# Hourglass attention and an ELU layer: a constant loaded ahead of v, v in 102-row transfers, two halves at the end of batch 0, and wider filling matmuls

## The chip, the cores and the metric

The kernel runs on one core of one Trainium2 chip. TensorE (PE) multiplies matrices into PSUM, VectorE (DVE), ScalarE (ACT) and GpSimd (POOL) do the elementwise work, SyncE (SP) and POOL issue transfers between DRAM and the core's memory. The metric is device time in microseconds for one execution. Profiles are of one execution each.

## The reference

The inputs q, k and v are 8 batches x 8 heads x 576 tokens x 64, float32. Each head has two attentions, added: one over tokens pooled by four, repeated back to 576, and one over a band of seven tokens. The result, laid out as 4608 x 512, goes through a two-matrix layer with ELU.

```python
q_d = q.reshape(B, H, Sd, factor, D).mean(axis=3)      # k_d, v_d likewise
out_up = np.repeat(sm_attn(q_d, k_d, v_d), factor, axis=2)
mask = np.abs(pos[:, None] - pos[None, :]) < factor    # factor = 4
scores = np.where(mask, scale * np.matmul(q, k.transpose(0, 1, 3, 2)), -1e9)
...
attn_out = out_up + np.matmul(softmax(scores), v)
h = x @ w_in                                           # x: 4608 x 512, w_in: 512 x 2048
return np.where(h > 0.0, h, np.exp(np.minimum(h, 0.0)) - 1.0) @ w_out
```

## The kernel before

Work is fp16 on PE with float32 sums. A batch is four pairs of heads. A pair is loaded (`load`, SP), cast to fp16 (`cast`, mostly POOL; the fp16 copies rotate through 4 buffers), transposed and pooled by matmuls (`transposes`), and multiplied to scores (`scores`): 576 tokens are six blocks of 96 queries, each against 102 keys (96 and three neighbours on either side), and the pooled 144. ACT takes the exponential, DVE applies the mask. `denominators` sums them by matmuls with an indicator matrix, DVE takes the reciprocal, and the reciprocals are then spread over 128 partitions: for batches 0 and 1 (`BY_PE`) by matmuls with the constant SEL (in the tile CC) and a copy by ACT; for the others by a transfer to DRAM and two back that repeat it (POOL). `pool_v` pools v by matmuls; `outputs` multiplies probabilities with v (L738) and pooled v (L746) into two banks, DVE multiplies by the reciprocals (xn, L755), and POOL, in batch 0 partly DVE, adds the local and the repeated pooled part into `xt`, blocks of 512 tokens that the layer reads.

The layer runs over nine blocks of 512 tokens: `mm1` (sixteen steps of four 512-column matmuls, L788; exponential on ACT, minimum and maximum on DVE) and `mm2` (four output rows, each in four steps of four matmuls, L811). A step needs its slice of w_in (five transfers w0 to w4) or of w_out (w5 to w8).

v lies in a tile of 102 partitions, so that block c of a head holds tokens 96c-3 to 96c+98 of its rows. For batches 1 to 7 POOL issues two halo transfers of 3 partitions x 48 blocks (L467) and two main ones of 96 partitions x 24 blocks (L422), which cast on the way. For batch 0, SP loads float32 (two halos L440 and L442, four main transfers of 96 partitions x 12 blocks L445) into a buffer lent by `gt`, and POOL casts (L450, vc00 to vc03).

The order of all this is written by a planner in the file (`Plan`): every operation has an engine, an assumed duration, a rank, and buffers; the planner runs a clock, lets each engine take the ready operation of lowest rank that has its buffers, and models transfers by an assumed rate. Ranks come from `PARAM`. The resulting order is then issued as it stands: on the chip each engine runs its list in that order, and waits where something is missing. Where the planner has nothing for PE before `FILL` = 37 us of its own clock, it puts a filling matmul (L337) of zeros into bank 7; these are instructions like others. The first 57 are ahead of the first transposes.

Every output, score or transpose takes a pair of banks ("two"): one of four pairs in batch 0, one of two pairs later. SP has eight transfers in flight at most; the next waits for the one eight before it.

```python
plan.zero = plan.op("DVE", 0.15, -99, lambda: nc.vector.memset(zero[:], 0.0), name="zero")
c_a = consts((("ONE", one_np), ("BY6", by6_np), ("VR", vr_np)), "CA", -60)
c_b = consts((("MASK", m2_np), ("IND", ind_np), ("SEED", seed_np)), "CB", -47.5)
c_c = consts((("SEL", sel_np),), "CC", -45.0)
```

Of the kernel before, what the change touches and what calls it, by code (L numbers as in the profile page):

```python
# [10 lines left out]
FP16 = mybir.dt.float16  # L11
# [7 lines left out]
NB, QB = 6, 96  # L19
# [66 lines left out]
class Plan:  # L86
# [63 lines left out]
    def run(self):  # L150
# [38 lines left out]
        while n < len(self.ops):  # L189
            for e, todo in ready.items():  # L190
                if busy[e] > now + 1e-9 or not todo and e != "PE":
                    continue
                if e == "SP" and len(lanes) >= 8 and lanes[-8].done is None:
                    continue
                full = e == "POOL" and sum(x[1] for x in queues["POOL"]) > self.depth
                todo.sort(key=lambda o: (o.rank, o.i))
                for o in todo:
                    if o.nbytes and full:
                        continue
                    got = []  # L200
                    for b in o.bufs:
                        if b.slot is None:
                            x = self._take(b, free)
                            if x is None:
                                break
                            self._hold(b, x, free)
                            got.append(b)
                    else:
                        break
                    for b in reversed(got):  # L210
                        self._drop(b, free, True)
                else:
# [54 lines left out]
    def emit(self):  # L267
        for o in self.order:
# [7 lines left out]
MOE_BANKS = {"hp": 3, "op": 2}  # L276
PARAM = dict(M0=43.0, P=36.0, LAG=0.84, LEAD=48.6, GAP=6.2, SC=2.7, DEN=29.4, OUT=8.8, OUTG=1.0, TV=18.4, LOAD=11.5,
             VLOAD=3.4, V1=2, warm=3.4, FILL=37.0, DEPTH=12.0, WI=-44.0, WO=43.8, WOG=2.5)


@with_exitstack
def kernel(
# [50 lines left out]
    plan.warm, plan.depth, plan.fill = PARAM["warm"], PARAM["DEPTH"], PARAM["FILL"]  # L333
    zero = sb.tile([128, 256], FP16, tag="zero", name="zero")

    def fill():
        nc.tensor.matmul(PS[:, 7, 384:512], zero[:, 0:128], zero[:, 128:256], start=True, stop=True)  # L337

# [76 lines left out]
    def load_v(b):  # L415
# [4 lines left out]
        def main(h):  # L420
            t = at(x)[3 : 3 + QB].rearrange("p j e c d -> p (j e c) d")
            nc.gpsimd.dma_start(  # L422
                out=t[:, 24 * h : 24 * h + 24, :],
                in_=bass.AP(tensor=a.tensor, offset=a.offset + 24 * h * QB * D, ap=[[D, QB], [QB * D, 24], [1, D]]),
            )

# [3 lines left out]
        if b == 0:  # L430
# [5 lines left out]

            def halos0(left):
                if left:
                    nc.vector.memset(flat()[0:3, 0:1, :], 0.0)
                    nc.sync.dma_start(out=flat()[0:3, 1:48, :], in_=blocks(1, 48, -3, 3))  # L440
                else:
                    nc.sync.dma_start(out=flat()[99:KW, :, :], in_=blocks(0, 48, QB, 3))  # L442

            def main0(j):
                nc.sync.dma_start(  # L445
                    out=flat()[3 : 3 + QB, 12 * j : 12 * j + 12, :], in_=blocks(12 * j, 12 * j + 12, 0, QB)
                )

            def cast0(j):
# [3 lines left out]

            hs = [op("SP", 0.45, r, lambda i=i: halos0(i), writes=[x32], nbytes=3 * 48 * 256, rate=100e3, name=f"vh{i}")
                  for i in range(2)]
            for j in range(NPAIR):
                o = op("SP", 0.45, r + 0.1, lambda j=j: main0(j), writes=[x32], nbytes=96 * 768 * 4, rate=205e3, packet=20, name=f"vm0{j}")
                plan.op("POOL", 0.85, r + 0.2, lambda j=j: cast0(j), writes=[x32, x], after=[o] + hs, name=f"vc0{j}")
                st.setdefault("vc", []).append(plan.ops[-1])
            st[b] = x  # L460
# [3 lines left out]

        def halo(p, tok, lo, hi):
            t = at(x)[p : p + 3].rearrange("p j e c d -> p (j e c) d")
            nc.gpsimd.dma_start(out=t[:, lo:hi, :], in_=blocks(lo, hi, tok, 3))  # L467

        def halos():
            t = at(x)  # L470
            if b == B - 1:
                nc.gpsimd.memset(t[96:KW, 3, 1, NB - 1, :], 0.0)
            halo(0, -3, 0, 48)
            halo(99, QB, 0, 47 if b == B - 1 else 48)

        pre = [wq[int(PARAM["V1"])]] if b == 1 else [wq[-1]]
        op("POOL", 1.6, r, halos, writes=[x], after=pre, nbytes=6 * 48 * 256, rate=60e3, packet=28, name=f"vh{b}")
        for h in range(2):
            op("POOL", 1.0, r + 0.1 + 0.1 * h, lambda h=h: main(h), writes=[x], after=pre, nbytes=96 * 24 * 256,
               rate=146e3, packet=28, name=f"vm{b}{h}")  # L480
# [4 lines left out]
    def weights(i):  # L485
        wi = i < 5
        if wi:
            lo, hi = WIC[i], WIC[i + 1]
            src = moe_w_in.rearrange("(c p) m -> p c m", p=128)[:, :, lo:hi]
            to, r, n = WI[:, :, lo:hi], PARAM["WI"] + 0.1 * i, hi - lo  # L490
        else:
            n = 4 * (i - 5)
            src = moe_w_out.rearrange("(c p) m -> p c m", p=128)[:, n : n + 4, :]
            to, r, n = WO[:, n : n + 4, :], PARAM["WO"] + PARAM["WOG"] * (i - 5), 512
        o = op("POOL", 1.3, r, lambda: nc.gpsimd.dma_start(out=to, in_=src), name=f"w{i}", after=[st["vc"][GATES[i]]],
               nbytes=128 * 16 * n, rate=330e3)
# [81 lines left out]
    def pool_v(b, j):  # L578
        s, r = st[b, j], out_rank(b) - PARAM["TV"] + j
        yv = st[b]  # L580
# [12 lines left out]
        w = Buf("vd")  # L593
        eng = "ACT" if b == 0 else "DVE"
        op(eng, 0.41, r + 0.1,
# [4 lines left out]
    def scores(b, j):  # L600
        s, r = st[b, j], late(b, j) + PARAM["SC"]
        m = b in SIX
# [38 lines left out]

    stR = {}

    def denominators(b, js):
        last = js[-1] == NPAIR - 1
        if b == 0:
            r = late(b, js[-1]) + PARAM["SC"] + 1.0
        else:
            r = M0 + P * b - PARAM["DEN"]
# [33 lines left out]
        if b in BY_PE:  # L683
# [3 lines left out]
            for j in js:  # L687
                w = Buf("two", b < EARLY)

                def spread(j=j, w=w):  # L690
# [9 lines left out]

                op("PE", 0.35, out_rank(b) - 1 + 0.1 * j, spread, reads=[c], writes=[w], after=[c_c], name=f"spr{b}{j}")
                op("ACT", 0.76, out_rank(b) - 0.9 + 0.1 * j,
                   lambda j=j, w=w: nc.scalar.copy(out=at(y)[:, j], in_=two(w, 0, 128, 0, GW)),
                   reads=[w], writes=[y], name=f"evr{b}{j}")
# [24 lines left out]
    def outputs(b, j):  # L729
        s, r = st[b, j], out_rank(b) + PARAM["OUTG"] * j  # L730
        x, vd, v16, y = s["ex"], s["vd"], st[b], stR[b, j]
        z, w = Buf("two", b < EARLY), Buf("xn")

        def go():
# [8 lines left out]
            for h in range(2):  # L743
# [142 lines left out]
```

## Time and profile before

| what | us |
|---|---|
| median of 3 runs (378.05, 380.81, 380.75) | 380.75 |
| the profiled execution | 379.33 |
| its span | 377.6 |
| PE busy (96% of the span) | 362.2 |
| of it mm1 and mm2 (1152 matmuls) | 146.8 + 144.8 |
| of it filling matmuls (173) | 19.3 |
| DVE, ACT, POOL busy | 226.0, 206.9, 144.1 |
| transfers | 44.06 MB, mean 117 GB/s |

A busy PE is not PE at its peak: matmuls are pipelined, so the duration of one (381 ns for 512 columns) is longer than its share of the time when many follow each other (0.86 us for four). PEclk is the clock that PE was granted, as a fraction. The DMA share is the mean busy share of 16 DMA engines; it can read over 1 where transfers overlap. Lines of the profile are `start, length, engine, line, operation, out<-in, count`, with the idle time before it and what ended it in brackets.

### The profile page before, as it was taken

The page shows a single profiled execution, that of the slowest core. Times are in us where ns is not written, and L with a number is a line of the kernel's source. Part 1 is how long each engine was busy: PE and PEld are TensorE (multiplying, and loading weights), DVE is VectorE, ACT ScalarE, POOL GpSimd, SP SyncE. Part 2 cuts the span into 40 slices and gives each one's busy share as a digit, 9 for nine tenths or more (in the row PEclk, how much of TensorE's full clock was granted, in tenths as well). Part 3 has the DMA queues.
Part 4 walks back from the last instruction along what each step waited for, and adds up shares of the span by engine and source line. Part 5 has one row for each costly group of instructions (what it writes and reads, how often), then busy time and mean ns, then how long its engine had stood idle before and what let it go on. Part 6 is the DMA issues. An engine that isn't in the chain of part 4 may idle for free.

```text
span 377.6 us, 9204 instructions
## 1 busy us (share of the span) xinstructions
PE 362.2 (96%) x3805; PEld 205.2 (54%) x3805; DVE 226.0 (60%) x407; ACT 206.9 (55%) x353; POOL 144.1 (38%) x225
## 2 busy tenths in 40 slices
PE   8969999999988999999999999999999999999995
PEld 8857855654644554555555555555555444444442
DVE  2623397847737665866576657665756675655530
ACT  2732489658452946494749474947494334443421
POOL 1282782199116813770387038703700240000000
PEclk9975699999998999999999999999999999999999
DMA  8999999929981997299729973924000401010012
GB/s 220 178 239 217 207 183 186 199 42 201 194 182 32 152 137 168 70 143 135 169 77 139 134 168 82 99 42 106 30 30 33 115 29 48 28 56 30 28 56 84
DMA packets 119740, 44.06 MB, mean 117 GB/s; under 512 B 105779, under 2 KB 113907, under 8 KB 119699
## 3 DMA queue, kind: packets, MB, share of 16 engines
q1 hardware_dynamic: 69971, 30.22, 35.3%
q0 software_dynamic: 49728, 13.26, 31.5%
q8 instruction: 29, 0.48, 0.5%
q14 instruction: 12, 0.10, 0.1%
HBM read 42.36 MB, written 9.66 MB: 138 GB/s over the span
## 4 chain that ended last, share of the span: by engine, by line
PE 83%; DMA 8%; DVE 3%; SPq 3%; ACT 2%; issue 1%; POOL 0%; DVEq 0%; ACTq 0%
PE bank L811 33%; PE bank L788 31%; PE bank L544 4%; PE bank L586 3%; PE bank L738 3%; DMA ld<-in_k_dram 3%; PE bank L658 2%; PE bank L612 2%; SPq L445 2%; DMA ld<-in_q_dram 2%; DMA rcb<-rd 2%; DMA CC<-CCc 1%; PE bank L337 1%; PE bank L746 1%; DVE e L796 1%; ACT ex L629 1%
## 5 line engine op out<-in xcount | busy, mean ns | idle before, releaser
L788 PE MATMUL bank<-xt,WI 128*128 128x512 f16 x576 | 146.8, 381 | 1.0 <-DVE gt L799 1.0
L811 PE MATMUL bank<-WO,gt 128*128 128x512 f16 x576 | 144.8, 381 | 0.0
L794 ACT ACTIVATE e<-bank 128x512 f16<-128x512 f32 x144 | 85.9, 600 | 89.8 <-PE bank L788 68.3
L799 DVE SCALAR_TENSOR_TENSOR gt<-bank,e 128x512 f16<-128x512 f32 x144 | 98.8, 689 | 5.2
L796 DVE TENSOR_SCALAR e<-e 128x512 f16<-128x512 f16 x144 | 54.4, 378 | 56.8 <-ACT e L794 56.2
L811 PEld LDWEIGHTS <-gt 128*128 128x128 f16 x576 | 53.6, 98 | 59.6 <-issue 0.3
L788 PEld LDWEIGHTS <-WI 128*128 128x128 f16 x576 | 52.7, 98 | 58.0 <-issue 2.6
L512 POOL CAST c<-ld 96x768 f16<-96x768 f32 x60 | 51.1, 868 | 46.8 <-issue 26.0
L629 ACT ACTIVATE ex<-bank 102x864 f16<-102x864 f32 x64 | 53.4, 887 | 21.8 <-PE bank L620 21.7
L771 POOL TENSOR_TENSOR xt<-xn 128x288 f16<-128x288 f16 (+8 forms) x92 | 44.8, 516 | 52.0 <-DVE xn L755 51.9
L637 DVE TENSOR_TENSOR ex<-ex,CB 102x1152 f16<-102x1152 f16 x32 | 25.1, 785 | 30.0 <-ACT ex L629 29.3
L755 DVE TENSOR_TENSOR xn<-bank,rcb 128x720 f16<-128x720 f32 x32 | 28.7, 903 | 15.3 <-DMA rcb<-rd 4.7
L826 ACT COPY os<-bank 128x512 f32<-128x512 f32 x36 | 21.1, 590 | 15.8 <-PE bank L811 15.7
L544 PEld LDWEIGHTS <-c 96*128 96x128 f16 x288 | 19.5, 99 | 10.2 <-issue 1.3
L559 ACT CAST qt<-bank 128x720 f16<-128x720 f32 x24 | 18.2, 757 | 10.8 <-PE bank L544 10.2
L544 PE MATMUL bank<-CA,c 96*128 96x120 f16 x288 | 23.0, 217 | 0.0
L708 POOL DMA_DIRECT2D rd<-rc x6 | 3.5, 582 | 49.1 <-DVE rc L681 49.1
L337 PE MATMUL bank<-zero 128*128 128x128 f16 x173 | 19.3, 280 | 1.9 <-DVE zero L340 1.1
L738 PE MATMUL bank<-ex,v 102*64 102x96 f16 x384 | 14.9, 218 | 4.2 <-DVE xn L755 3.7
L738 PEld LDWEIGHTS <-v 102*64 102x64 f16 x384 | 11.0, 116 | 13.0 <-issue 12.6
L570 ACT CAST kt<-bank 128x576 f16<-128x576 f32 x24 | 15.5, 646 | 4.2 <-PE bank L544 2.8
L596 DVE CAST vd<-bank 72x256 f16<-72x256 f32 x28 | 11.5, 416 | 9.9 <-PE bank L586 9.9
(47 smaller groups left out, 265.0 us busy)
## 6 DMA issues: line engine op xcount, KB each, us to landing
ld<-in_q_dram SPq DMA_DIRECT2D x32, 288.0 KB, 5.5
ld<-in_k_dram SPq DMA_DIRECT2D x32, 288.0 KB, 6.1
out_dram<-os SPq DMA_DIRECT2D x36, 256.0 KB, 2.1
rcb<-rd POOLq DMA_DIRECT2D x12, 360.0 KB, 5.1
v<-in_v_dram POOLq DMA_DIRECT2D x14, 288.0 KB, 7.6
WO<-in_moe_w_out_dram POOLq DMA_DIRECT2D x4, 512.0 KB, 16.0
WI<-in_moe_w_in_dram POOLq DMA_DIRECT2D x3, 512.0 KB, 16.7
gt<-in_v_dram SPq DMA_DIRECT2D x4, 288.0 KB, 8.2
```

The source lines that it names most:

```text
L512: f(out=at(y)[:], in_=at(x)[:].rearrange("p e c d -> p c e d"))
L544: nc.tensor.matmul(o, t[:, c, :, :], C["ONE"], start=True, stop=True)
L629: lambda e=e: nc.scalar.activation(out=at(x)[:, e], in_=two(sc[e], 0, KW, 0, HB + SD), func=AF.Exp, scale=SCALE),
L637: nc.vector.tensor_tensor(out=a, in0=a, in1=mk, op=AB.mult)
L738: nc.tensor.matmul(PS[64 * e : 64 * e + 64, z.slot[0] + c // 3, QB * (c % 3) : QB * (c % 3) + QB], v_[:, j, e, c, :], ex[:, e, c // 3, QB ...
L755: lambda: nc.vector.tensor_tensor(out=at(w)[:], in0=two(z, 0, 128, 0, GW), in1=at(y)[:, j], op=AB.mult),
L771: (nc.vector if eng == "DVE" else nc.gpsimd).tensor_tensor(out=at(xt(t))[:, j, o : o + n - a], in0=ln, in1=gn, op=AB.add)
L788: nc.tensor.matmul(one(h, 0, 128, 0, TBLK), WI[:, dc, 128 * fc : 128 * fc + 128], at(x)[:, dc, :], start=(dc == 0), stop=(dc == DMC - 1),)
L794: op("ACT", 0.55, r, lambda: nc.scalar.activation(out=at(e)[:], in_=one(h, 0, 128, 0, TBLK), func=AF.Exp), reads=[h], writes=[e], name=f"e ...
L796: op("DVE", 0.36, r, lambda: nc.vector.tensor_scalar(out=at(e)[:], in0=at(e)[:], scalar1=1.0, scalar2=-1.0, op0=AB.min, op1=AB.add), reads ...
L799: op("DVE", 0.69, r, lambda: nc.vector.scalar_tensor_tensor(out=at(gt)[:, fc, :], in0=one(h, 0, 128, 0, TBLK), scalar=0.0, op0=AB.max, in1 ...
L811: nc.tensor.matmul(one(z, 0, 128, 0, DM), at(gt)[:, fc, 128 * tt : 128 * tt + 128], WO[:, fc, :], start=(fc == 0), stop=(fc == FCN - 1),)
```

## The change

Eight edits, all but the last in what the planner is given:

- CC is ranked directly behind CB, ahead of the last pair of q and k of batch 0 and of v.
- v of batch 0: the four main transfers start three tokens earlier and fill partitions 0 to 95 (first block left out of the first); one transfer of 6 partitions x 47 blocks brings the rest, two small ones the first block. v of batches 1 to 7: no halos; two transfers of 102 partitions x 24 blocks (the last batch's last block apart, by one more).
- Batch 0's end: the spreads of pairs 0 and 1 come ahead of the scores of pair 3; the four v-poolings stand together, the copies of the first two on DVE instead of ACT; the outputs of pairs 0 and 1 come ahead of the second half of the denominators, those of pairs 2 and 3 behind it.
- Filling matmuls have 256 columns instead of 128; the planner takes 0.112 us for each instead of 0.107. 158 instead of 173 are issued, 54 instead of 57 of them ahead of the first transposes.
- POOL's transfers over 400 KB wait until its queue holds less than 2 us of work (12 before, and any transfer then). w3 goes behind the first four adds of batch 0, w4 behind the rest of them and two casts, w5 to w8 behind casts of batch 2.
- The reciprocals' trip through DRAM is modelled by bytes instead of fixed delays.
- Ranks: see PARAM. Besides, xn now enters the planner as a writer of `rcb`.
- The order that results: scores of batch 1's first pair follow the first two mm1 steps instead of preceding them; the v-poolings of batch 1 stand directly behind its denominators, ahead of its spreads; the first mm2 step follows mm1's sixteenth instead of its ninth. For batch 2, four blocks of mm1 and mm2 stand between its first and second output, and nine between the second and the third.

```diff
-                    if o.nbytes and full:
+                    if o.nbytes > 400000 and full:
...
-                        o = Op("PE", 0.107, 0, self.filler, "fill")
+                        o = Op("PE", 0.112, 0, self.filler, "fill")
...
-PARAM = dict(M0=43.0, P=36.0, LAG=0.84, LEAD=48.6, GAP=6.2, SC=2.7, DEN=29.4, OUT=8.8, OUTG=1.0, TV=18.4, LOAD=11.5,
-             VLOAD=3.4, V1=2, warm=3.4, FILL=37.0, DEPTH=12.0, WI=-44.0, WO=43.8, WOG=2.5)
+PARAM = dict(M0=33.0, P=36.0, LAG=0.84, LEAD=50.2, GAP=5.6, SC=2.5, DEN=29.4, OUT=8.8, OUTG=0.9, TV=15.0, LOAD=22.0,
+             VLOAD=14.6, V1=2, warm=3.4, FILL=37.0, DEPTH=2.0, WI=-44.0, WO=41.2, WOG=2.1)
...
-    zero = sb.tile([128, 256], FP16, tag="zero", name="zero")
+    zero = sb.tile([128, 384], FP16, tag="zero", name="zero")
...
-        nc.tensor.matmul(PS[:, 7, 384:512], zero[:, 0:128], zero[:, 128:256], start=True, stop=True)
+        nc.tensor.matmul(PS[:, 7, 256:512], zero[:, 0:128], zero[:, 128:384], start=True, stop=True)
...
-    c_c = consts((("SEL", sel_np),), "CC", -45.0)
+    c_c = consts((("SEL", sel_np),), "CC", -47.0)
...
+    def spr_rank(b, j):
+        if b == 0:
+            return -30.5 + 0.1 * j if j < 2 else -27 + 0.1 * j
+        return out_rank(b) - 1 + 0.1 * j
...
         def main(h):
-            t = at(x)[3 : 3 + QB].rearrange("p j e c d -> p (j e c) d")
...
+            t = at(x)[:].rearrange("p j e c d -> p (j e c) d")
+            hi = 24 * h + 24
...
+            nc.gpsimd.dma_start(out=t[:, 24 * h : hi, :], in_=blocks(24 * h, hi, -3, KW))
...
+            def first():
+                nc.vector.memset(flat()[0:3, 0:1, :], 0.0)
+                nc.sync.dma_start(out=flat()[3:99, 0:1, :], in_=blocks(0, 1, 0, QB))
+
+            def last():
+                nc.sync.dma_start(out=flat()[96:KW, 1:48, :], in_=blocks(1, 48, 93, 6))
+                nc.sync.dma_start(out=flat()[99:KW, 0:1, :], in_=blocks(0, 1, QB, 3))
...
-                nc.sync.dma_start(
-                    out=flat()[3 : 3 + QB, 12 * j : 12 * j + 12, :], in_=blocks(12 * j, 12 * j + 12, 0, QB)
-                )
+                lo = max(12 * j, 1)
+                nc.sync.dma_start(out=flat()[0:QB, lo : 12 * j + 12, :], in_=blocks(lo, 12 * j + 12, -3, QB))
...
-        op("POOL", 1.6, r, halos, writes=[x], after=pre, nbytes=6 * 48 * 256, rate=60e3, packet=28, name=f"vh{b}")
...
-            to, r, n = WI[:, :, lo:hi], PARAM["WI"] + 0.1 * i, hi - lo
+            to, r, n = WI[:, :, lo:hi], PARAM["WI"] if i < 3 else -25.0, hi - lo
...
-        s, r = st[b, j], out_rank(b) - PARAM["TV"] + j
+        s, r = st[b, j], out_rank(b) - PARAM["TV"] + j if b else -29.5 + 0.1 * j
...
-        eng = "ACT" if b == 0 else "DVE"
+        eng = "ACT" if b == 0 and j > 1 else "DVE"
...
-            r = late(b, js[-1]) + PARAM["SC"] + 1.0
+            r = late(b, js[-1]) + 2.8 if js[0] == 0 else -28.5
...
-               reads=[c], writes=[d], name=f"spo{b}").lag = 3.0
+               reads=[c], writes=[d], name=f"spo{b}", nbytes=36864, rate=100e3, packet=30)
...
-                op("POOL", 0.8, r + 1.1, lambda e=e: spread(e), reads=[d], writes=[y], name=f"spi{b}{e}").lag = 4.0
+                op("POOL", 0.8, r + 1.1, lambda e=e: spread(e), reads=[d], writes=[y], name=f"spi{b}{e}", nbytes=64 * 4 * 1440, rate=200e3, packet=90)
...
-        s, r = st[b, j], out_rank(b) + PARAM["OUTG"] * j
+        s, r = st[b, j], out_rank(b) + PARAM["OUTG"] * j if b else (-29 if j < 2 else -26) + 0.1 * j
...
-           reads=[z, y], writes=[w], name=f"xn{b}{j}")
+           reads=[z], writes=[w, y], after=[evr[b, j]] if b in BY_PE else y.writers, name=f"xn{b}{j}")
```

More of the change, by code (lines that the diff above doesn't have):

```diff
@@ L420, in main @@
         def main(h):
-            t = at(x)[3 : 3 + QB].rearrange("p j e c d -> p (j e c) d")
-            nc.gpsimd.dma_start(
-                out=t[:, 24 * h : 24 * h + 24, :],
-                in_=bass.AP(tensor=a.tensor, offset=a.offset + 24 * h * QB * D, ap=[[D, QB], [QB * D, 24], [1, D]]),
-            )
+            t = at(x)[:].rearrange("p j e c d -> p (j e c) d")
+            hi = 24 * h + 24
+            if b == B - 1 and h == 1:
+                hi -= 1
+                nc.gpsimd.memset(t[96:KW, hi, :], 0.0)
+                nc.gpsimd.dma_start(out=t[0:99, hi : hi + 1, :], in_=blocks(hi, hi + 1, -3, 99))
+            nc.gpsimd.dma_start(out=t[:, 24 * h : hi, :], in_=blocks(24 * h, hi, -3, KW))
         def blocks(lo, hi, tok, n):
@@ L435, in flat @@
                 return t.rearrange("p (c d) -> p c d", d=D)
[L437 to L442, printed above, removed]
+            def first():
[4 more added lines that the diff above has]
+                nc.sync.dma_start(out=flat()[99:KW, 0:1, :], in_=blocks(0, 1, QB, 3))
             def main0(j):
-                nc.sync.dma_start(
-                    out=flat()[3 : 3 + QB, 12 * j : 12 * j + 12, :], in_=blocks(12 * j, 12 * j + 12, 0, QB)
-                )
+                lo = max(12 * j, 1)
+                nc.sync.dma_start(out=flat()[0:QB, lo : 12 * j + 12, :], in_=blocks(lo, 12 * j + 12, -3, QB))
             def cast0(j):
@@ L452, in cast0 @@
                 )
-            hs = [op("SP", 0.45, r, lambda i=i: halos0(i), writes=[x32], nbytes=3 * 48 * 256, rate=100e3, name=f"vh{i}")
-                  for i in range(2)]
+            hs = [
+                op("SP", 0.9, r, last, writes=[x32], nbytes=6 * 48 * 256, rate=150e3, name="vh0"),
+                op("SP", 0.45, r, first, writes=[x32], nbytes=96 * 256, rate=150e3, name="vh1"),
+            ]
             for j in range(NPAIR):
-                o = op("SP", 0.45, r + 0.1, lambda j=j: main0(j), writes=[x32], nbytes=96 * 768 * 4, rate=205e3, packet=20, name=f"vm0{j}")
+                o = op("SP", 0.45, r + 0.1, lambda j=j: main0(j), writes=[x32], nbytes=96 * 768 * 4, rate=175e3, packet=20, name=f"vm0{j}")
                 plan.op("POOL", 0.85, r + 0.2, lambda j=j: cast0(j), writes=[x32, x], after=[o] + hs, name=f"vc0{j}")
+                plan.ops[-1].lag = 0.8
                 st.setdefault("vc", []).append(plan.ops[-1])
@@ L463, in load_v @@
             return
[L465 to L474, printed above, removed]
         pre = [wq[int(PARAM["V1"])]] if b == 1 else [wq[-1]]
-        op("POOL", 1.6, r, halos, writes=[x], after=pre, nbytes=6 * 48 * 256, rate=60e3, packet=28, name=f"vh{b}")
         for h in range(2):
-            op("POOL", 1.0, r + 0.1 + 0.1 * h, lambda h=h: main(h), writes=[x], after=pre, nbytes=96 * 24 * 256,
+            op("POOL", 1.0, r + 0.1 + 0.1 * h, lambda h=h: main(h), writes=[x], after=pre, nbytes=KW * 24 * 256,
                rate=146e3, packet=28, name=f"vm{b}{h}")
@@ L494, in weights @@
             to, r, n = WO[:, n : n + 4, :], PARAM["WO"] + PARAM["WOG"] * (i - 5), 512
-        o = op("POOL", 1.3, r, lambda: nc.gpsimd.dma_start(out=to, in_=src), name=f"w{i}", after=[st["vc"][GATES[i]]],
+        o = op("POOL", 0.8, r, lambda: nc.gpsimd.dma_start(out=to, in_=src), name=f"w{i}", after=[st["vc"][GATES[i]]],
                nbytes=128 * 16 * n, rate=330e3)
@@ L600, in scores @@
     def scores(b, j):
-        s, r = st[b, j], late(b, j) + PARAM["SC"]
+        s, r = st[b, j], late(b, j) + (PARAM["SC"] if b else 2.7)
         m = b in SIX
@@ L640, in scores @@
         s["ex"] = x
-    stR = {}
+    stR, evr = {}, {}
     def denominators(b, js):
@@ L699, in spread @@
                         )
-                op("PE", 0.35, out_rank(b) - 1 + 0.1 * j, spread, reads=[c], writes=[w], after=[c_c], name=f"spr{b}{j}")
-                op("ACT", 0.76, out_rank(b) - 0.9 + 0.1 * j,
+                op("PE", 0.35, spr_rank(b, j), spread, reads=[c], writes=[w], after=[c_c], name=f"spr{b}{j}")
+                evr[b, j] = op("ACT", 0.76, spr_rank(b, j),
                    lambda j=j, w=w: nc.scalar.copy(out=at(y)[:, j], in_=two(w, 0, 128, 0, GW)),
```

## The prediction

> **What bounds the kernel now.** I read the page first, then the chain of waits, then busy time by window, then the engine timeline at the two places the windows point to. The page says the tensor engine is the bound almost throughout; what it does not say is whether it is busy with useful work. Two lines of the 40 slices (9.4 us each) do:
>
> ```profile
> PE   8969999999988999999999999999999999999995
> PEclk9975699999998999999999999999999999999999
> ```
>
> The clock is low only in slices three to five (19 to 47 us) and a little in slice thirteen. By windows (PE, weight loads, DVE, ACT, POOL busy, granted clock, DMA share, GB/s):
>
> ```profile
> 20.00:22.00 2.00, 0.00 (x0) 0.00 (x0) 0.37 (x2) 1.66 (x2) 1.61 (x3) 1.00 1.20 256
> 22.00:24.00 2.00, 0.36 (x5) 0.37 (x6) 0.57 (x1) 0.00 (x0) 1.51 (x2) 0.94 1.08 234
> 24.00:26.00 2.00, 2.00 (x21) 1.78 (x19) 0.00 (x0) 0.12 (x1) 2.00 (x4) 0.50 1.07 258
> ...
> 112.00:114.00 2.00, 0.00 (x0) 0.00 (x0) 0.00 (x0) 0.11 (x1) 0.00 (x0) 1.00 0.35 119
> 114.00:116.00 2.00, 0.85 (x22) 0.68 (x22) 1.81 (x3) 0.00 (x0) 0.82 (x2) 0.98 0.01 3
> 116.00:118.00 2.00, 2.00 (x11) 1.04 (x10) 2.00 (x4) 0.00 (x0) 2.00 (x5) 0.50 0.00 0
> ```
>
> Twice the tensor engine stands still for over 3.5 us, and each time the clock is 0.50 afterwards: from 24 to 44.5 us, and from 116 to about 119.5. From 120 to 360 us it is busy for 240.00 of 240 us, so whatever is lost before 120 us is lost for good, and nothing but that is to be had. The chain of waits and the PE timeline name the two causes (start, length, what):
>
> ```profile
> 16.91 1.81 SPq L445
> 18.76 4.83 DMA CC<-CCc
> ...
> 107.93 6.13 DMA rcb<-rd
> ```
> ```profile
> 1.06 6.01 PE L337 MATMUL bank<-zero 128*128 128x128 f16 x57 [1.06 <-DVE zero L340]
> 18.30 1.11 PE L337 MATMUL bank<-zero 128*128 128x128 f16 x17 [0.41 <-DVE rc L681]
> 23.64 0.71 PE L696 MATMUL bank<-rc,CC 32*128 32x144 f16 x6 [3.69 <-DMA CC<-CCc]
> 31.78 1.57 PE L337 MATMUL bank<-zero 128*128 128x128 f16 x13
> 115.15 0.45 PE L738 MATMUL bank<-ex,v 102*64 102x96 f16 x12 [3.67 <-DVE xn L755]
> ```
>
> The first spread sits in PE's queue waiting for its constant CC, which SP issues only after four v transfers; everything behind it, fillers too, waits. The second stop is batch 2's outputs waiting for the reciprocals' trip through DRAM. The first mm1 starts at 44.64 us, after 20 us at half clock.
>
> **Part by part.**
>
> *CC ahead of v.* It is issued after CB, so by about 5 us. CB took 8.5 us to land (at 12.6); CC is right behind it with 160 KB at some 230 GB/s, so there by 13.5 us, before the first spread (its reciprocal ends at 18.25). The 3.69 us stop goes. The last q and k of batch 0 (the cast that waits for them starts at 15.81) and v are pushed back by these 0.7 us; v ends where CC ended, at about 23.6.
>
> *v of batch 0 without halos.* Two transfers of 3 rows x 48 pieces become one of 6 x 47, one of 3 and one of 96. The four main issues took 9.50 us on SP, so the queue was full and it, not SP, is the limit. The casts start at 18.63, 19.72, 21.14 and 23.29, about 1.6 us for 72 pieces on each of 16 engines. If a row stays on one engine, the halos put 95 pieces on three engines and now 48 on six: 0 to 1.0 us sooner. I take 0, since nothing shows which engines; the last cast ends at about 24.5.
>
> *Fillers of 256 columns.* This has a price. Four 512-column matmuls take 0.86 us at full clock, 216 ns each; so a 256-column one is 108 ns at full and 216 at half clock. The first 57 of 128 columns took 6.01 us, 105 ns each, against 65 for the 17 at 18.30: they ran at half speed, though the clock column shows 1.00 there. Of the 54 new ones, 27 fit into the 5.84 us that the old ones took to 6.9 us, and 27 x 0.108 = 2.9 us follow. The first transposes start at 9.8 instead of 6.9. The bounds are 0 (full speed from the start) and 5.8 us (half speed throughout).
>
> *From there to the first mm1.* In the new order PE runs without a hole: 10 transposes at 0.60, 4 scores at 0.50, 2 half denominators at 1.0, 4 spreads at 0.36, 4 v-poolings at 0.32 (1.28 for two at half clock), 4 outputs at 0.42, and 104 fillers at 0.108: 6.0 + 2.0 + 2.0 + 1.4 + 1.3 + 1.7 + 11.2 = 25.6 us, with 0.4 for hand-overs 26.0; mm1 at 35.8. Is anything later than that? PE reaches the first v-pooling at 9.8 + 4.8 + 2.0 + 1.0 + 0.7 + 75 x 0.108 = 26.4, the casts end at 24.5: covered by 1.9 us. The two copies moved to DVE (0.42 each) stand behind the last mask, due at about 26, and end at 27.2, where PE gets to outputs at 27.7. POOL's adds end at 35. So 44.64 becomes 35.8; one scores step of batch 1 (0.5) is moved behind mm1. Gain 8.3 us.
>
> *Weights on POOL.* w1 and w2 follow one cast more, w3 and w4 come behind adds (issue at about 32 and 38 instead of 25.5 and 26.3). The queue held the five for 11.6 to 19.5 us, w4 landing at 45.8; mm1 needs its part (the thirteenth block, 18 us after the first in the trace) at 35.8 + 18 = 54. Nothing lost. The output weights go behind casts of batch 2, about 55 to 68 us, one every 3 to 4 us, needed from 64 on; at 7 us to landing for the first (44.19 before, behind w4) they are in time by 1 to 3 us. I take 0, up to 3.
>
> *v of batches 1 to 7.* Four POOL issues (2 x 0.77 + 2 x 1.20 us) become two; POOL has room, so the 1.5 us are worth nothing. What matters is landing. For batch 1 the second transfer is behind a cast that waits for a buffer of the third pair, so at about 48 us; the v-pooling of batch 1 moved ahead of the spreads and needs it at 35.8 + 24 = 60. Twelve us, where the trace shows:
>
> ```profile
> v<-in_v_dram POOLq DMA_DIRECT2D x14, 288.0 KB, 7.6
> ...
> rd<-rc POOLq DMA_DIRECT2D x6, 36.0 KB, 1.8
> ...
> v<-in_v_dram POOLq DMA_DIRECT2D x13, 18.0 KB, 3.6
> ```
>
> and 12.5 as the longest, in just this stage. A row of 3 partitions with 144 pieces takes twice as long as one of 128 partitions with 128 pieces and twice the bytes: how the rows divide over the engines counts. For 102 rows no row exists. Bounds: 0 (7.6 us) and 11 us (the third rival). I take 1.0 us, nearest to the 96-row transfers.
> The Trainium skill, DMA: Bandwidth & Descriptors (Why a DMA increments its semaphore by 16 and not by 1), says a transfer uses the largest number of engines up to 16 that divides the rows, which is 16 for 96 and 6 for 102, with an exception that gives some POOL copies 16. By the rule the third rival's 390 would come out; by the exception (7 rows on most engines) the sum would stand.
>
> *Reciprocals of batch 2.* In the new order ten mm blocks of 0.87 us, four v-poolings and a scores step stand on PE between batch 2's denominators and its first output (10.5 us), and thirteen blocks and two transposes between that and the output that needs a bank back from xn (11.9), where there were three blocks. Less 1.1 for DVE's reciprocal, PE needs the reciprocals 21 us after they are made. They took 14.4 us, from 99.67 to landing at 114.06. The 3.67 us stop goes, and with it the half clock: 2 us at 0.50 and 2 at 0.67 cost 1.0 + 0.7. Gain 5.4 us. What is late next: batch 3, where PE has only about the 8.3 us of that trip (140.11 to 148.44); 0 to 2, I take 0.5.
>
> *Between.* Without an mm2 block among them, the 16 mm1 go at ACT's pace (per pair 2 x 0.89 + 1.9 + 4 x 0.60 = 6.1 us against 5.2 on PE): 1.0 lost, 0 to 2.
>
> Sum: 8.3 + 5.4 - 1.0 - 0.5 - 1.0 = 11.2 us. The profiled execution took 379.33 (span 377.6), the median of the runs is 380.75: 368.1 and 369.5. I say 369.
>
> **Rivals.**
>
> *The clock falls all the same.* If v's casts end 3.5 us later than PE gets to them (at 30 instead of 24.5), PE stops there and all to mm1 runs at half clock; from 27 to 36 that is some 9 us more, less what the fillers covered: about 377. For it: the DMA share is over 1.0 all that time, and SP sees v later. Against: v moves no more bytes.
>
> *The reciprocals' stop stays*, since the trip in POOL's queue now has a v transfer between its two halves: 5.4 are not gained, 374.4. Against: the 21 us, which would leave 7 for it.
>
> *Slower: v of batch 1 lands on few engines.* From the rows above, 48 pieces on an engine cost 3.6 - 1.8 us more than 8: 46 ns each. 144 pieces give 6.6 + 1.8 = 8.4, near the 7.6 seen. If the rows were divided evenly, 102 would go to 6 engines (17 each): 408 pieces give 20.6 us. Then v of batch 1 at 69, PE stopped for 9 us and at half clock after (1.7); batch 2, with 12 us as well, the same: 369 + 2 x 10.7 = 390. It decides from about 12 us to landing; each us over that is one lost. Against: in the quiet stages the 3-row transfers landed in 2.6 us, which makes a piece much cheaper.
>
> *It does less than it says*: with all fillers at half speed at the start and the output weights 3 us late, 369 + 2.9 + 3 = 375.
>
> **How the numbers follow.** Forecast 0.60, at 363.5 to 372.5: down by 2.9 with the first fillers at full speed, 1.5 with no new waits and 1.0 with v sooner; up by 3 with the fillers or the output weights at their dear end. The clock 0.10, the reciprocals 0.09, few engines 0.11, less than it says 0.10. A difference below 1% (3.8 us) can hardly be told from none here. Faster by over 1% (under 377): 0.60 + 0.09, half of the clock's 0.10, and 0.06 of the last, the rest of which meets another loss: 0.80. Within 1%: 0.05 + 0.04 = 0.09. Slower: 0.11. The range, 363.5 to 376.5, holds all that lies under 377.
>
> **What would show it.** Right: no PE stop over 1 us and a clock of 1.00 from 10 to 120 us; first transposes at 8.5 to 10; mm1 at 34 to 37; no stop at 111; v of batch 1 in under 12 us. Wrong: the L586 group or L811 waiting for a DMA near 60 to 70 us, a half clock in slices three to five, or xn waiting for rcb in batch 2 or 3.

## The result, and the profile after

The change makes the kernel slower, by more than it was forecast to gain.

| kernel | median us | lowest to highest | ratio to before, 95% |
|---|---|---|---|
| before (same chip, 4 runs) | 379.80 | 378.05 to 380.81 | |
| changed (4 runs) | 395.00 | 393.71 to 400.51 | 1.039 [1.032, 1.047] |

The slowest run of the changed kernel, 400.51 us, was in a slower state of the chip and is not in the ratio.

The profiled execution took 393.71 us (span 391.7), 14.4 more than the one of before. The first mm1 starts at 41.21 instead of 44.64, so 3.4 us are gained by then. From there to the end of the last matmul it takes 346.7 us instead of 329.05: 17.7 are lost in the part that the change was least expected to touch. On the page, PE and its clock in 40 slices (9.8 us each):

```profile
PE   8998997899699999599979899999999999999996
PEclk9998999699999999799989999999999999999999
```

Of the low clock in slices three to five one dip is left, in slice 4 (counted from 1). New are the holes of PE in slices 7, 11, 17 and 21; but for slice 11, a low clock stands in the same slice or the next. The PE timeline says what stands there; its last bracket is the idle time ahead of the line and what ended it:

```profile
34.19 2.15 PE L337 MATMUL bank<-zero 128*128 128x256 f16 x10 [1.69 <-DVE rc L679]
...
67.90 0.97 PE L584 MATMUL bank<-v,CA 102*72 102x128 f16 x12 [2.03 <-DMA v<-in_v_dram]
...
71.20 1.87 PE L809 MATMUL bank<-WO,gt 128*128 128x512 f16 x4 [1.39 <-DMA ld<-in_q_dram]
...
104.50 0.86 PE L584 MATMUL bank<-v,CA 102*72 102x128 f16 x12 [3.42 <-DMA v<-in_v_dram]
...
162.21 0.69 PE L736 MATMUL bank<-ex,v 102*64 102x96 f16 x12 [4.14 <-DVE xn L753]
...
201.07 0.47 PE L542 MATMUL bank<-CA,c 96*128 96x120 f16 x6 [2.30 <-DVE xn L753]
```

(Two lines have gone from the code, so L586, L738, L788, L811 and L755 of before are L584, L736, L786, L809 and L753 here.) v of batch 1 is late at 68 us and v of batch 2 at 104; the reciprocals of batches 3 and 4 are late at 162 and 201; where there was a stop of 3.67 us for batch 2's reciprocals at 115, there is none. The line at 71.20 is a first mm2 step. The page names a load of q, but the first of the output weights, issued by POOL at 59.1, landed at 71.1, and that is what this step needs.

With one of 1.20 us at 223 the stops behind the first mm1 add up to 14.5 us where there were 3.7, which is 10.8 more. The half clock at these places adds up to 17.1 us where there were 3.4; 2.9 of the 17.1 lie inside the stops at 71 and 162. A microsecond at half clock loses at most half of itself, so this costs up to (17.1 - 2.9 - 3.4) / 2 = 5.4 more. Together that is 16.2 of the 17.7. By windows (columns as before) this is how such a place looks:

```profile
66.00:68.00 2.00, 0.10 (x2) 0.10 (x3) 0.25 (x1) 1.58 (x2) 0.00 (x0) 1.00 1.28 191
68.00:70.00 2.00, 1.81 (x24) 1.35 (x24) 1.51 (x4) 0.38 (x1) 0.00 (x0) 0.63 1.22 197
70.00:72.00 2.00, 0.80 (x2) 0.36 (x3) 0.80 (x2) 1.04 (x2) 0.00 (x0) 0.50 1.22 201
```

PE has nothing to do, the DMA engines are busy throughout, and POOL does nothing; it had issued the second v transfer of batch 1 by 55.6 us. The wait is for the transfer, not for its issue. In the page's DMA parts a queue has its packets, MB and share, and an issue its count, KB each and median us to landing. First a queue of the kernel before:

```profile
q0 software_dynamic: 49728, 13.26, 31.5%
```

The same queue after, and two rows of issues:

```profile
q0 software_dynamic: 97760, 13.46, 38.1%
...
v<-in_v_dram POOLq DMA_DIRECT2D x13, 306.0 KB, 14.5
WO<-in_moe_w_out_dram POOLq DMA_DIRECT2D x4, 512.0 KB, 13.6
```

q0 is POOL's queue. It moves 1.5% more bytes in twice as many packets, and v takes 14.5 us to land where the main transfers took 7.6. POOL is held longer by each issue too, 2.54 us instead of 1.20. What goes the same way behind v pays as well: the chain of waits (start, length, what) has

```profile
88.12 16.34 DMA v<-in_v_dram
...
155.42 5.71 DMA rcb<-rd
...
187.50 5.72 DMA rd<-rc
...
194.14 5.84 DMA rcb<-rd
```

rd<-rc moves 36 KB and had a median of 1.8 us. Batch 4's is issued at 187.5 while the v transfer of 174.1 is on its way; v lands at 193.0 and rd<-rc at 193.2. Batch 3's was issued at 148.3 behind one of 135.8 that landed at 153.5, and landed at 154.5.

### The profile page after: what moved, and what is told of

It reads as the page before. It is cut to its first block, busy times and chain, and to the rows that moved or that the text cites. A ratio compares the mean times of both kernels' runs of the same rounds, so it can differ in the third digit from the quotient of the medians.

```text
span 391.7 us, 9156 instructions
## 1 busy us (share of the span) xinstructions
PE 367.8 (94%) x3790; PEld 203.7 (52%) x3790; DVE 233.6 (60%) x409; ACT 207.8 (53%) x351; POOL 155.2 (40%) x212
## 3 DMA queue, kind: packets, MB, share of 16 engines
q0 software_dynamic: 97760, 13.46, 38.1%
## 4 chain that ended last, share of the span: by engine, by line
PE 73%; DMA 14%; DVE 5%; issue 4%; ACT 2%; POOL 1%; DVEq 0%; ACTq 0%; POOLq 0%
PE bank L809 29%; PE bank L786 24%; PE bank L337 5%; DMA v<-in_v_dram 4%; DMA ld<-in_q_dram 3%; PE bank L542 3%; DMA rcb<-rd 3%; PE bank L736 3%; DMA out_dram<-os 2%; PE bank L610 2%; PE bank L584 2%; DVE e L794 2%; DMA rd<-rc 1%; PE bank L656 1%; DVE xn L753 1%
## 5 line engine op out<-in xcount | busy, mean ns | idle before, releaser
L809 PE MATMUL bank<-WO,gt 128*128 128x512 f16 x576 | 148.2, 387 | 3.1 <-DMA ld<-in_q_dram 1.4
L786 PE MATMUL bank<-xt,WI 128*128 128x512 f16 x576 | 145.1, 380 | 1.6 <-DVE gt L797 1.5
L794 DVE TENSOR_SCALAR e<-e 128x512 f16<-128x512 f16 x144 | 58.9, 410 | 59.6 <-ACT e L792 59.1
L809 PEld LDWEIGHTS <-gt 128*128 128x128 f16 x576 | 53.8, 99 | 62.8 <-issue 5.7
L786 PEld LDWEIGHTS <-WI 128*128 128x128 f16 x576 | 53.8, 98 | 62.4 <-issue 4.0
L769 POOL TENSOR_TENSOR xt<-xn 128x288 f16<-128x288 f16 (+8 forms) x92 | 46.0, 527 | 47.3 <-DVE xn L753 47.0
L627 ACT ACTIVATE ex<-bank 102x864 f16<-102x864 f32 x64 | 53.5, 889 | 10.8 <-PE bank L618 10.6
L753 DVE TENSOR_TENSOR xn<-bank,rcb 128x720 f16<-128x720 f32 x32 | 28.7, 903 | 31.2 <-PE bank L744 19.0
L432 POOL DMA_DIRECT2D v<-in_v_dram x14 | 35.5, 2538 | 7.9 <-issue 7.8
L337 PE MATMUL bank<-zero 128*128 128x256 f16 x158 | 24.2, 307 | 3.2 <-DVE rc L679 2.1
L542 PE MATMUL bank<-CA,c 96*128 96x120 f16 x288 | 21.9, 216 | 2.5 <-DVE xn L753 2.3
L542 PEld LDWEIGHTS <-c 96*128 96x128 f16 x288 | 18.4, 97 | 11.0 <-issue 2.8
L337 PEld LDWEIGHTS <-zero 128*128 128x128 f16 x158 | 16.2, 109 | 7.3 <-issue 2.4
L584 PE MATMUL bank<-v,CA 102*72 102x128 f16 x192 | 14.3, 221 | 5.4 <-DMA v<-in_v_dram 5.4
L736 PE MATMUL bank<-ex,v 102*64 102x96 f16 x384 | 14.9, 217 | 4.1 <-DVE xn L753 4.1
## 6 DMA issues: line engine op xcount, KB each, us to landing
v<-in_v_dram POOLq DMA_DIRECT2D x13, 306.0 KB, 14.5
```

Source lines behind the costliest of these rows:

```text
L337: nc.tensor.matmul(PS[:, 7, 256:512], zero[:, 0:128], zero[:, 128:384], start=True, stop=True)
L432: nc.gpsimd.dma_start(out=t[:, 24 * h : hi, :], in_=blocks(24 * h, hi, -3, KW))
L542: nc.tensor.matmul(o, t[:, c, :, :], C["ONE"], start=True, stop=True)
L627: lambda e=e: nc.scalar.activation(out=at(x)[:, e], in_=two(sc[e], 0, KW, 0, HB + SD), func=AF.Exp, scale=SCALE),
L753: lambda: nc.vector.tensor_tensor(out=at(w)[:], in0=two(z, 0, 128, 0, GW), in1=at(y)[:, j], op=AB.mult),
L769: (nc.vector if eng == "DVE" else nc.gpsimd).tensor_tensor(out=at(xt(t))[:, j, o : o + n - a], in0=ln, in1=gn, op=AB.add)
```

## The experiments

The first theory was that the rows are the cause: 102 is 6 x 17, so that v of batches 1 to 7 goes over few engines in long runs, everything in POOL's queue waits, and PE's stops follow. The rival was that the loss lies in the rest of the change, its order at the end of batch 0, its wide fillers and its later weights, with v only one of several late things. Each run below was timed beside runs of the kernel before: their median was 378.82 us for the first four experiments and 376.60 for the next four, and the last stands beside a single run of 377.20.

**The changed kernel with 112 rows.** Ten rows more than anybody reads; 112 is 16 x 7. VW is 112 and KW stays 102; what reads v takes rows 0 to 101, and those lines are left out here.

```diff
-        "v16": many("v16", [KW, NPAIR, 2, NB, 64]),
+        "v16": many("v16", [VW, NPAIR, 2, NB, 64]),
...
-            nc.gpsimd.dma_start(out=t[:, 24 * h : hi, :], in_=blocks(24 * h, hi, -3, KW))
+            nc.gpsimd.dma_start(out=t[:, 24 * h : hi, :], in_=blocks(24 * h, hi, -3, VW))
```

> The changed kernel, order untouched, but each v transfer of batches 1 to 7 has 112 rows instead of 102 (ten more rows of following tokens that nothing reads; 112 is 7 x 16). Theory 1, the row count: 102 rows are what makes a v transfer slow, so although 10% more bytes move, landing falls from 14.5 us to 8 to 9, POOL's issue of one from 2.5 us to about 1.3, packets in POOL's queue from 97,760 to about 53,000, and the stops at 68, 104, 162 and 201 us with the half clock behind them go: 395 - 2.0 - 3.4 - 4.1 - 2.3 - 1.4 - 7.0 for the half clock = about 375. Theory 2, the order: v is slow because of where it is issued, among loads and weights; 10% more bytes make it worse, 395 or more, landing 14.5 us or more.

Measured: 371.75 us, 0.983 [0.979, 0.986]. One number in a transfer's shape, with 10% more bytes, is worth 22 us (1.039 less 0.983, times 379). v landed in 6.4 us (8 to 9 expected), POOL's queue held 44,160 packets (53,000 expected), and no stop behind the first mm1 was over 0.31 us except one of 1.93 for batch 3's reciprocals at 147 us.

**The kernel before with 102 rows.** Only the halos and the 96-row transfers of batches 1 to 7 are replaced.

```diff
-            t = at(x)[3 : 3 + QB].rearrange("p j e c d -> p (j e c) d")
+            t = at(x)[:].rearrange("p j e c d -> p (j e c) d")
...
+            nc.gpsimd.dma_start(out=t[:, 24 * h : hi, :], in_=blocks(24 * h, hi, -3, KW))
...
-            halo(0, -3, 0, 48)
-            halo(99, QB, 0, 47 if b == B - 1 else 48)
+            pass
```

> The kernel before, with its v transfers of batches 1 to 7 made as the changed kernel makes them: two of 102 rows, no halos; nothing else changed. Theory 1: landing rises from 7.6 us to 13 to 15, POOL's issue of one from 1.2 to 2.5 us, packets in POOL's queue from 49,728 to about 97,000; the reciprocals of batch 2, behind v in the queue, land 4 to 8 us later, so 384 to 388. Theory 2: landing stays at 7 to 8 us and the time at 380 or a little below.

Measured: 400.03 us, 1.054 [1.049, 1.059], so this part alone costs 21 us in the old order (400.03 less 378.82), more than expected. q0 has 97,760 packets again and v lands in 13.8 us. Most of the price came at one place. The chain of waits of this kernel:

```profile
110.84 9.82 DMA rd<-rc
...
121.89 5.58 DMA rcb<-rd
```

and its PE timeline:

```profile
128.56 0.69 PE L736 MATMUL bank<-ex,v 102*64 102x96 f16 x12 [13.97 <-DVE xn L753]
```

The old stop of batch 2 grew from 3.67 to 13.97 us, and the half clock there from 3.41 to 13.65. The other stops over 1 us are one for v at 105.72 (2.05) and three of 1.47 to 1.72 at 169, 186 and 227. The long stop is mostly a late start. DVE had the reciprocals at 100.54, 0.9 us later than before, but POOL issued their transfer (rd<-rc) at 110.84 instead of 100.19, as its timeline shows:

```profile
97.99 2.49 POOL L427 DMA_DIRECT2D v<-in_v_dram  x1 [5.76 <-issue]
105.98 2.47 POOL L427 DMA_DIRECT2D v<-in_v_dram  x1 [5.50 <-issue]
...
110.84 0.61 POOL L706 DMA_DIRECT2D rd<-rc  x1
```

Two v transfers stand ahead of it in POOL's list, and POOL stood idle for 5.76 and 5.50 us before issuing them. Each went out 0.3 to 0.4 us after an earlier v transfer had landed (at 97.63 and 105.67), with two of 102 rows under way until then. The changed kernel does the same at 97.49 and 104.78, behind landings at 97.11 and 104.46. That POOL waits for these landings is read from the times; the profile names no releaser. From issue to the last landing the trip then took 16.6 us instead of 13.9, of which 9.82 for 36 KB behind v. In the changed kernel the reciprocals stand ahead of the second of these v transfers in POOL's list, their transfer was issued at 101.51, and PE needs them later.

**The changed kernel with fillers of 128 columns**, in the same order and number, and the same with 112 rows.

```diff
-        nc.tensor.matmul(PS[:, 7, 256:512], zero[:, 0:128], zero[:, 128:384], start=True, stop=True)
+        nc.tensor.matmul(PS[:, 7, 384:512], zero[:, 0:128], zero[:, 128:256], start=True, stop=True)
```

> The changed kernel, order and number of filling matmuls untouched, each of 128 columns instead of 256. If the wide fillers delay the start as worked out (54 of them at half speed first), the first transposes start at about 7 instead of 10.1 us and the first mm1 2 to 4 us earlier than 41.4; the time 391 to 393. If the narrow ones let the clock fall somewhere, it is not below 395.

> Both: 112-row v transfers and fillers of 128 columns in the changed kernel's order. If both costs are separate they add: about 372, below the 380 of the kernel before. Theory 2: about 392.

Measured: 396.33 us, 1.046 [1.041, 1.051], and 371.41 us, 0.980 [0.976, 0.984], neither apart from its twin with 256 columns. So the wide fillers are no part of the loss. The first 54 end in 5.49 us instead of 8.95, and the prediction had charged 2.9 for this; but the wait for the reciprocal is then longer, on the PE timeline of the first of the two:

```profile
31.42 1.22 PE L337 MATMUL bank<-zero 128*128 128x128 f16 x10 [4.26 <-DVE rc L679]
```

and the clock is at half for 10.24 us, from 29.82 on with 102 rows and from 28.48 with 112. mm1 starts at 38.99 and 39.02. With 112 rows it starts at 38.76 with wide fillers: what these cost at the start, they give back in the clock. With 102 rows the narrow ones bring mm1 2.2 us sooner, within the 2 to 4 expected, but from there to the last matmul it takes 351.3 us instead of 346.7; the stop for v at 68 is 3.65 instead of 2.03. The costs of rows and fillers add, as expected (371.41, for about 372).

**The kernel before with CC ahead of v.**

```diff
-    c_c = consts((("SEL", sel_np),), "CC", -45.0)
+    c_c = consts((("SEL", sel_np),), "CC", -47.0)
```

> The kernel before with one edit: CC ranked behind CB, ahead of v. Theory 1 (the stop was what threw the clock to half): the 3.69 us stop at 23.6 us and the 20 us at half clock go, the first mm1 comes at 36 to 38 instead of 44.9 us, the time is 370 to 373 against 379. Theory 2 (the fillers of 128 columns leave PE idle enough for the clock to fall anyway, as in e3 from 30 us on): the clock is at half for 10 us or more before the first mm1, which comes at 40 to 43; 375 to 378.

Measured: 372.66 us, 0.988 [0.980, 0.995]. The stop of 3.69 us is gone and mm1 starts at 38.63, 6.0 earlier than in the profile of before. But with narrow fillers and two stops of 0.71 and 1.22 us behind them the clock still fell, at about 28, for 10.24 us: the time is that of the first theory, the clock that of the second. This one rank gives as much as the whole change with 105 rows (0.989, next).

**The changed kernel with 105 rows**, 15 x 7, the same edit with VW = 105: is it a multiple of 16 that matters, or the length of the run on one engine?

> e1 with 105 rows instead of 112. If the rows are dealt out in equal shares over the largest number of engines up to 16 that divides them (105 = 15 x 7, 112 = 16 x 7, 102 = 6 x 17), a transfer has 16 x 7 places for each of 24 blocks as with 112, POOL's queue has the same 44,160 packets, landing is 6 to 7 us and the time 371 to 372. If it is multiples of 16 that are fast, 105 is like 102: some 98,000 packets, 14 us to landing, 394 to 396.

Measured: 372.05 us, 0.989 [0.981, 0.996]; 44,160 packets exactly as with 112 rows, though 7 rows less, and v lands in 6.0 us. So it isn't multiples of 16: packets and time go with the run of 7.

**The kernel before with 112 rows**, the second edit with 112 for 102.

> The kernel before with v of batches 1 to 7 in two transfers of 112 rows and no halos, order untouched. By the count of places (16 x 7 x 24 for each of the two, against 16 x 6 x 24 for two and 16 x 48 for each of two halos) POOL's queue has 14 x 784 packets less minus what 112 rows add, some 5,500 less than 49,728; the reciprocals of batch 2 land 1 to 3 us sooner, the stop at 111 us is shorter, and the time 375 to 378. If fewer transfers are worth nothing and bytes count, 379 to 381.

Measured: 375.86 us, 0.998 [0.994, 1.001]: not to be told from before. Leaving out the halos, with 112 rows, is worth nothing here that can be told; POOL's queue is shorter by 5,568 packets, and the stop at 111 us is 2.25 instead of 3.67.

**105 rows, and the second half of batch 0's denominators earlier.** In the changed kernel 17 fillers follow these denominators. Seven run, and the eighth waits 1.69 us (34.19 in the timeline above) for DVE's reciprocal. The fillers write columns 256 to 511 of bank 7; the wait says that the sums stand in the same bank, in other columns. DVE is at two xn and two adds until 33.05. The edit lets the denominators go ahead of the outputs of pairs 0 and 1, and so DVE's reciprocal ahead of xn:

```diff
-            r = late(b, js[-1]) + 2.8 if js[0] == 0 else -28.5
+            r = late(b, js[-1]) + 2.8 if js[0] == 0 else -29.15
```

> e6 with the second half of batch 0's denominators ranked ahead of the outputs of pairs 0 and 1 instead of behind them (rank -29.15 for -28.5), so that its reciprocal is not queued on DVE behind two xn and two adds. The 1.7 us stop at 33.5 us and the fillers behind it go, the first mm1 comes at 36 to 37.5 instead of 39, and the time is 369 to 370.5. If something else is late then (the adds, v's copies), the first mm1 stays at 38 to 39 and the time at 371 to 372.

Measured: 370.07 us, 0.982 [0.975, 0.989], the lowest median of all, and faster than either kernel; it isn't told apart from the ones with 112 or 105 rows alone. Of the 1.69 us stop, 0.26 are left. mm1 starts at 38.57, later than expected (36 to 37.5). On its page the clock has no hole left, and PE only that of batch 3's reciprocals (1.52 us at 147):

```profile
PE   8999999999999998999999999999999999999995
PEclk9999999999999999999999999999999999999999
```

**The changed kernel with 110 rows**, 11 x 10: a size between, run once.

> The changed kernel with v of batches 1 to 7 in transfers of 110 rows: a size between the cheap ones (105 and 112: 7 rows on each of 15 or 16 engines, 168 blocks of a row on each) and the dear one (102: 17 rows on each of 6, 408 blocks). 110 is 11 x 10, so 240 blocks on each of 11 engines. Theory 1 (what a v transfer costs is the number of blocks that its busiest engine carries, and the queue is filled up to 16 times that number): 335 blocks x 16 places x 3 rows more than with 105, 16,080, so 60,240 packets in POOL's queue; landing on the line between 6.0 us at 168 and 14.5 us at 408 blocks, 8.6 us at the median; issue 1.6 us; time 371 to 375. Theory 2 (a cliff: transfers are cheap or dear according to whether all, or nearly all, engines take part): 11 engines are on the dear side, landing 12 us or more and 385 or more. Rival to the packet count: 44,160 as with 105 and 112 if there is another reason for that number.

The DMA rows of this kernel:

```profile
q0 software_dynamic: 60240, 13.64, 36.6%
...
v<-in_v_dram POOLq DMA_DIRECT2D x13, 330.0 KB, 8.9
```

and of the one with 105 rows:

```profile
q0 software_dynamic: 44160, 13.37, 32.1%
...
v<-in_v_dram POOLq DMA_DIRECT2D x13, 315.0 KB, 6.0
```

60,240 packets, as expected to the last one; landing 8.9 us for 8.6 expected, issue 1.73 us for 1.6; 375.91 us, just over the 371 to 375 expected, and not to be told from the single run of before (377.20). So there is no cliff. If the rows are dealt out evenly as above, the busiest engine gets 24 x 7, 24 x 10 or 24 x 17 pieces of a row per transfer of 24 blocks: 168, 240, 408, and v lands in 6.0 to 6.4, 8.9 and 14.5 us. That is (14.5 - 6.2) / (408 - 168) = 35 ns a piece, in a queue that other transfers share.

What the packets are can be read from their sizes. Those of 128 bytes, one row of a block, number 34,269 before and after. All that has been added, 48,032, are packets of 4 bytes. From 105 to 102 rows, 335 blocks x 16 x (17 - 7) = 53,600, which is exactly 97,760 - 44,160: the queue is charged 16 places for every row of the run, with data in six of them and 4 bytes in the other ten. The 4-byte packets agree: 335 x 17 x 10 = 56,950, and 685 more, as many as there are with 112 rows. That they fill the places of engines without data is read out of these counts; which engine carried what isn't in the trace.

Whether the long runs on a few engines or the filling takes the time isn't tested, since the two grow together in every size tried. The packets' own times speak for the few engines. A 128-byte packet takes 32 ns on average with 102, 105 and 112 rows and 34 with 110, and a 4-byte one 10 to 13. How many of 128 bytes are under way at once differs: during 95% of the time that there are any, at most 40 with 112 rows, 38 with 105, 30 with 110 and 17 in the changed kernel (20 in the old order with 102). These go nearly as 16, 15, 11 and 6.

## Why the prediction was wrong

*The step that failed* is "v of batches 1 to 7": "For 102 rows no row exists. Bounds: 0 (7.6 us) and 11 us (the third rival). I take 1.0 us, nearest to the 96-row transfers." The row to be near to was the halo's, 3 rows on as many engines. By the ratios to before, 1.039 with 102 rows against 0.983 with 112 and 0.989 with 105, that step cost 22 and 19 us, and 21 in the old order. My upper bound of 11 us was one batch's wait; the rival's two, 2 x 10.7, are what was lost. The margin itself was read well: 12 us were forecast between issue and need of batch 1's second transfer, and it was 12.8 (53.08 to 65.87); the landing took 14.8. All three signs of being wrong came: waits for a DMA at 68 and 71 us, a half clock in slice four, and xn waiting for rcb in batch 3.

*The third rival had the right mechanism, and its number by luck.* It gave 390, with a chance of 0.11; 393.7 and 395.0 came. Its pieces were too dear (46 ns, against 35), so v landed in 14.5 and not in 20.6 us, and the stops for v were 2.03 and 3.42 us, not 9 and 9. That it still came out nearly right is because it also left out the other half: the output weights (1.39 us) and the reciprocals of batches 3 and 4 (4.14 and 2.30), which wait in the same queue behind v, and the half clock behind each. What I held against it, that 3-row transfers land in 2.6 us in quiet stages, does not speak against it: 48 pieces at 35 ns are 1.7 us.

The Trainium skill, DMA: Bandwidth & Descriptors (Why a DMA increments its semaphore by 16 and not by 1), says that the largest number up to 16 that divides the rows gets the work: 6 for 102, 11 for 110, 15 for 105. The packet counts of all four sizes agree with that rule. By the exception that it names, 16 engines and rows rounded up, 102 rows would have been runs of 7 and 44,160 packets; the trace has 97,760, so it doesn't hold for this transfer. The last batch's transfer of 99 rows and one block does fit it: the 685 small packets are 16 for each of POOL's 42 transfers and 13 more, which is 16 x 7 - 99. (The old kernel's 9,603 are 16 for each of 55 transfers and 13 for each of 671 halo blocks of three rows, 16 - 3.)

*CC ahead of v* held: it landed at 12.8 (13.5 forecast), the 3.69 us stop is gone, and the old kernel with this alone gains 1.2%.

*v of batch 0 without halos* held: the last cast ends at 24.85 (24.5).

*Fillers of 256 columns* held: 54 took 8.95 us, and the first transposes start at 9.92 (9.8). That close a fit is partly luck: in the other runs with wide fillers they took 8.00 to 8.98, as the clock rose at 5.1 to 7.1 us.

*First mm1 at 35.8* did not. It came at 41.21. The v-poolings were at 28.2 and not 26.4, by small hand-overs that the 0.4 did not cover: 1.8. The filler waited 1.69 for the reciprocal, and a spell of 3.41 us at half clock followed; where the eighth run took both away, mm1 started 2.6 us sooner, at 38.57. That leaves about 1.0 between v-poolings and mm1. I had listed what PE does and missed that a filler, too, has to wait: what stands in the bank that it writes must have been read.

*Weights*: taken at 0, up to 3. A stop of 1.39 us in the changed kernel, and none over 0.35 at that place with 105 or 112 rows. The step was right but for its queue.

*Reciprocals of batch 2* held: that stop is gone in every run with the new order. With 112 and 105 rows the trip took 14.6 and 14.2 us, of the 21 that the prediction gave it. In the changed kernel it took 25.0 (99.22 to 124.18), and that there was no stop is partly luck: the output that needs a bank back from xn came at 126.36, and without the 3.42 us that PE had stood for v at 104 it would, by estimate, have come at 122.9, ahead of xn (from 124.30 on). *What is late next, batch 3*, was 2.0 us with good rows, the dear end of 0 to 2, where I took 0.5; the eighth run has 1.52 there and 0.75 at 227.

*Between*, 1.0: with 105 rows, from the first mm1 to the last matmul it takes 326.6 us, 2.4 less than before. The old stop and its clock are 5.4 less, the new stops 2.7 more, which leaves 0.3: less than forecast.

With 105 rows, then, mm1 is 5.2 us sooner instead of 8.3, and the rest 2.4 shorter instead of 2.9 (5.4 - 1.0 - 0.5 - 1.0): 7.6 us (379.33 - 371.76), two thirds of the 11.2 forecast. These are single executions, and not timed side by side; by the ratio to the runs beside it, 0.989, the gain is about 4 us (376.60 to 372.05 in the medians). The rows alone turned the change round: without them it gains. But CC's rank alone gains as much (372.66), so that the other steps together are worth anything in time isn't shown.

## What to carry to other kernels

Where a transfer that POOL issues gets a new number of rows, divide it: in these runs landing and packets followed the rows over their largest divisor up to 16, times the blocks, and three useless rows (105 for 102) brought landing from 14.5 to 6.0 us. When one transfer becomes slow, go through all that is queued behind it, down to the smallest, and through what stands behind the next one in the list of the engine that issues it. And a matmul that only fills time still waits for whoever reads the bank it writes.

## What the runs showed of the hardware that was not expected

A queue's packets can nearly double at nearly the same bytes (49,728 to 97,760, with 1.5% more): the 34,269 packets of a row of v stood among 57,635 of 4 bytes, 48,032 more than before. And POOL, with two transfers of 102 rows under way, stood idle for 2.7 to 5.8 us before the next, which went out 0.3 to 0.4 us after one had landed.

The clock's spells at half speed are whole multiples of 3.41 us in all profiles taken: 3.41, 6.83, 10.24, 13.65 and 20.48. The same 1.69 us stop of the filler cost one spell in the changed kernel, and none in the runs with 112, 105 and 110 rows. The Trainium skill, TensorE: Matmul & The Clock Gate (What's actually happening), has the clock decided over windows of 3413 ns that run freely and don't start with the kernel. That agrees with the lengths; that the stop fell otherwise into the windows of those three runs is likely, but wasn't tested.

Fillers of 128 columns were not enough to hold the clock in any run: between 8 us and the first mm1 it was at half for 10.24 us or more in all six kernels with them, and for 3.41 us or not at all in the five with 256 columns. In five of the six a stop of 2.89 us or more stands there as well; only in the old kernel with CC ahead of v are the stops short (0.71 and 1.22), so that the width alone does it rests on that run.
